# The gathers of segments 5 to 10 issued one segment earlier, in front of the scatters they stood behind

## The chip, the cores and the metric

The kernel runs on one core of a Trainium2 chip. The metric is the device time of one execution in microseconds (us); the median of three runs of the kernel before is 499.98 us (493.82 to 501.89). The core has a matrix engine (TensorE, PE in the profile, with its weight loads as PEld), a vector engine (VectorE, DVE), a scalar engine (ScalarE, ACT), GpSimd (POOL) and a synchronising engine (SP). Each engine works through its own program in order and waits on semaphores for the others. DMA transfers are issued by SP (queue 1 in the profile) and by GpSimd (queue 0) and run beside the engines.

## The reference

Inputs are attention operands q, k, v of shape (4, 8, 576, 64), a router, eight experts and a convolution layer. Cut to what matters:

```python
def reference(...):
    x = windowed_and_dilated_attention(q, k, v)        # (4, 576, 512), 2304 tokens in all
    # MoE: each token has ONE expert e (arg max of x @ w_gate, or the expert of the token before it)
    h = np.maximum(x[b, s] @ w1[e], 0.0)               # w1[e]: 512 x 1024
    out[b, s] = p[e] * (h @ w2[e])                     # w2[e]: 1024 x 512
    # last layer: 5-tap causal convolution as a gate, two 512 x 512 products
    return (sigmoid(conv(out)) * (out @ w_val)) @ w_out
```

Which tokens belong to which expert is only known at run time. So the kernel has to collect the rows of each expert's tokens before the expert's products and to put the results back to the tokens' places afterwards.

## The kernel before, in words

The kernel has three stages: attention with routing (to about 180 us of the profiled execution), the experts (to about 381 us, with the first of them overlapping the attention), and the convolution layer with its two products.

**Segments.** The expert stage is cut into eleven segments, 0 to 10, listed in `SEGS` (line 39) as expert, first slot and number of tokens: 256, 208, 96, 288, 272, 240, 224, 192, 176, 160 and 256 tokens. The loop at lines 1247 to 1282 runs segments 2 to 8; segments 9 and 10 follow it. A segment goes through these steps:

- `gather` (line 305): GpSimd issues one indirect DMA (line 311) for every 128 tokens, from the tensor `xD` in HBM into a tile `xg`. There are four buffers for `xg` (line 220), used in rotation; a buffer is free once TensorE has transposed what it held. Segment 4 has three such tiles, the segments from 5 on have two.
- `turn_x` (line 315): TensorE transposes the tile (line 323, result `xt`), ScalarE and VectorE split it into a high and a low half-precision part, `xh` and `xl` (lines 324, 325).
- `up` (line 328): the first product, eight blocks `h` of three-part sums (line 342), each taken out of PSUM by ScalarE (`hh`, line 344) and VectorE (`hl`, line 346).
- `down` (line 355): the second product, for some tokens by `yf` (line 391, 512 columns) and for the others by `y` (line 375), whose result is turned back by `turn_y` (line 404).
- `send_y` (line 350): ScalarE writes a tile `yr` (three buffers), and GpSimd issues an indirect DMA that scatters its rows into `yD` in HBM (line 353). All scatters write the same tensor `yD`, so each waits on GpSimd for the one ahead of it to land.

**What sets the order.** The order is written out by hand: `up` and `down` are generators that stop after each piece, and the loop counts the pieces with `n` (0 to 7 in `up`, from 8 in `down`) and puts other work between them. In segment g the loop issues the gather of segment g + 1 at n = 0 (line 1254) and transposes it from n = 9 (lines 1270 to 1273), that is in the middle of segment g's `down`. In segment 8 the gather of segment 10 follows that of segment 9 at n = 1, and segment 10 is transposed at the end of the segment (line 1280). The scatters of segment g are issued late in its `down`, just ahead of the next segment's n = 0, so in GpSimd's program each gather stands behind all scatters of the segment before.

**Beside it** run the weights. Eight tiles of 512 KB per expert are fetched by SP into six staging buffers (`wst`, `fetch_w`, line 243) and split by ScalarE (`wh`, line 259) and VectorE (`wl`, line 264), in segment g for segment g + 1; a fetch starts when `wl` has freed its buffer. `late` (from line 1162) prepares the last layer's weights in small steps on VectorE and ScalarE.

Of the kernel before, what the change touches and what calls it, by code (L numbers as in the profile page):

```python
# [157 lines left out]
def attention_moe_conv_kernel(ctx: ExitStack, tc: tile.TileContext, q, k, v, w_gate, w_local, w1, w2, w_val, conv_w, w_out, consts, out):  # L158
# [84 lines left out]
    def fetch_w(k, i, ev):  # L243
        staged.append(staged.pop(0))
        st = staged[-1].tile([P, 1024], F32, tag="wst", name=f"wst{k}_{i}")
        if i < 4:
            nc.sync.dma_start(out=st, in_=w1[bass.ds(ev, 1), i * P : i * P + P, :].rearrange("o p f -> p (o f)"))
        else:
            f0 = (i - 4) * 2 * P
            nc.sync.dma_start(out=st.rearrange("p (a d) -> p a d", a=2), in_=w2[bass.ds(ev, 1), f0 : f0 + 2 * P, :].rearrange("o (a p) d -> p (o a) d", p=P))  # L250
        wf[k, i] = st

    def split_a(k, i):
        w = pools["w1" if i < 4 else "w2"][turn_no[k]]
        st = wf[k, i]
        wh = w.tile([P, 1024], F16, tag="wh", name=f"wh{k}_{i}")
        wl = w.tile([P, 1024], F16, tag="wl", name=f"wl{k}_{i}")
        wt[k, i] = wh, wl
        A.activation(out=wh, in_=st, func=AF.Copy, scale=SW)  # L259

    def split_b(k, i):
        wh, wl = wt[k, i]
        st = wf.pop((k, i))
        V.scalar_tensor_tensor(out=wl, in0=st, scalar=SW, in1=wh, op0=ALU.mult, op1=ALU.subtract)  # L264
# [29 lines left out]
    def tiles_of(n):  # L294
        return [(t0, min(P, n - t0)) for t0 in range(0, n, P)]

    def cols_of(g, which):
        k, t0, n = SEGS[g]
        if k in (0, 2):
            ix = idx[k, t0 > 0][which]  # L300
            return lambda t: ix[:, t : t + 1]
        ix = (idx8, sidx8)[which]
        return lambda t: ix[:, k, t0 + t : t0 + t + 1]

    def gather(g, n=None, col=None, tiles=None):
        if col is None:
            n, col = SEGS[g][2], cols_of(g, 0)
        r = []
        for t0, m in tiles_of(n)[tiles or slice(None)]:
            x = xg.tile([P, D], F32, tag="xg", name=f"xg{g}_{t0}")  # L310
            G.indirect_dma_start(out=x[:m], out_offset=None, in_=xD[0 : 2 * S if g in (0, 1) else N, :], in_offset=bass.IndirectOffsetOnAxis(ap=col(t0 // P)[:m], axis=0))
            r.append(x)
        return r

    def turn_x(g, xs, n=None, pool=None):
        n = n or SEGS[g][2]
        xh = (pool or act).tile([P, 4, n], F16, tag="xh", name=f"xh{g}")
        xl = (pool or act).tile([P, 4, n], F16, tag="xl", name=f"xl{g}")
        xts[g] = (xh, xl)
        for (t0, m), x in zip(tiles_of(n), xs):  # L320
            ps = trp.tile([P, 4, P], F32, tag="tr", name=f"xt{g}_{t0}")
            for cc in range(4):
                T.transpose(ps[:, cc, :m], x[:m, cc * P : cc * P + P], ident[:m, :m])
            A.activation(out=xh[:, :, t0 : t0 + m], in_=ps[:, :, :m], func=AF.Copy, scale=SX)
            V.scalar_tensor_tensor(out=xl[:, :, t0 : t0 + m], in0=ps[:, :, :m], scalar=SX, in1=xh[:, :, t0 : t0 + m], op0=ALU.mult, op1=ALU.subtract)
            yield

    def up(g, k=None, n=None, pool=None, halves=False):
        if n is None:
            k, _, n = SEGS[g]  # L330
        xh, xl = xts.pop(g)
        hh = (pool or pools["h"]).tile([P, 8, n], F16, tag="hh", name=f"hh{g}")
        hl = (pool or pools["h"]).tile([P, 8, n], F16, tag="hl", name=f"hl{g}")
        hts[g] = (hh, hl)
        for fc in range(8):
            fs = slice(fc * P, fc * P + P)
            ps = pools["hp"](f"h{g}_{fc}")
            q = 0
            for cc in range(4):
                wh, wl = wt[k, cc]  # L340
                for w, x in ((wh, xh), (wh, xl), (wl, xh)):
                    T.matmul(ps[:, :n], lhsT=w[:, fs], rhs=x[:, cc, :], start=q == 0, stop=q == 11)  # L342
                    q += 1
            A.activation(out=hh[:, fc, :], in_=ps[:, :n], func=AF.Relu)  # L344
            yield
            V.scalar_tensor_tensor(out=hl[:, fc, :], in0=ps[:, :n], scalar=0.0, in1=hh[:, fc, :], op0=ALU.max, op1=ALU.subtract)  # L346
            if halves:
                yield
# [70 lines left out]
    def drain(g):  # L419
        for _ in g:  # L420
            pass


    if True:
# [554 lines left out]
        vq, xq, evs, xs = [], [], {}, [[], []]  # L979
# [182 lines left out]
    def last_layer(pool):  # L1162
        parts = [(conv_w, KT, None)]
        for src, th, tl, sc in ((w_val, wv_h, wv_l, SVAL), (w_out, wo_h, wo_l, SOUT)):
            parts += [(src[cc * P : cc * P + P, :], P, (th[:, cc, :], tl[:, cc, :], sc)) for cc in range(4)]
        raws = []

        def load(n):
            src, rows, _ = parts[n]
            raw = pool.tile([P, 2 * D if wide else D], I32 if wide else F32, tag="lraw", name=f"lraw{n}", bufs=2)[:rows]  # L1170
            nc.sync.dma_start(out=raw, in_=src.bitcast(I32) if wide else src)
            raws.append(raw)

        load(0)
        for n, (_, rows, to) in enumerate(parts):
            yield
            w32 = raws[n]
            if wide:
                steps = from64(pool, w32, rows, D, f"{n}")
                for m in range(6):  # L1180
                    next(steps)
                    if m == 2 and n + 1 < len(parts):
                        load(n + 1)
                    yield
                w32 = next(steps)
            elif n + 1 < len(parts):
                load(n + 1)
            yield
            if to is None:
                yield  # L1190
                yield
                ps = trp.tile([P, 4, KT], F32, tag="tr", name="cwp")
                for cc in range(4):
                    T.transpose(ps[:, cc, :], w32[:, cc * P : cc * P + P], ident[:KT, :KT])
                V.tensor_copy(out=cw, in_=ps)
                continue
            th, tl, sc = to
            A.activation(out=th, in_=w32, func=AF.Copy, scale=sc)
            yield
            V.scalar_tensor_tensor(out=tl, in0=w32, scalar=sc, in1=th, op0=ALU.mult, op1=ALU.subtract)  # L1200
# [9 lines left out]
    with tc.manual_schedule():  # L1210
# [9 lines left out]
        for t, _ in enumerate(chain(rest_of(first, begun), down(0, pool=pools["y0"]), up(1), down(1)), 45):  # L1220
# [5 lines left out]
            n = t - 45 - sum(at >= 45 for at in UP)  # L1226
# [4 lines left out]
            if t == LAST[1]:  # L1231
                xs3 = gather(3)
# [4 lines left out]
            if t == LAST[3]:  # L1237
                turn = turn_x(2, xs2)
# [4 lines left out]
        r3ctx.close()  # L1243
        last_y = turn_y(1)
        late = last_layer(lw)
        xs = xs3
        for g in range(2, 9):
            kn, kf = SEGS[g + 1][0], SEGS[min(g + 2, 9)][0]
            for n, _ in enumerate(chain(up(g), down(g))):
                if 0 < n < 4:  # L1250
                    next(last_y, None)
                if n in (0, 2, 4) and g == 2:
                    fetch_w(3, 3 + n // 2, evs[3])
                if n == 0 and g > 2:
                    xs = gather(g + 1)
                if n == 1 and g == 8:
                    xs = xs + gather(10)
                if g > 2:
                    if n % 2:
                        split_b(kn, n // 2)  # L1260
                        i = n // 2 + 6
                        if i < 8:
                            fetch_w(kn, i, evs[kn])
                        elif g < 8:
                            fetch_w(kf, i - 8, evs[kf])
                    else:
                        split_a(kn, n // 2)
                for _ in range(LATE[g - 2][n]):
                    next(late, None)
                if n == 9:  # L1270
                    turn = turn_x(g + 1, xs)
                if n in (9, 11, 13):
                    next(turn, None)
                if g == 2 and n == 8:
                    rest()
                if g == 3 and n == 4:
                    weights_of()
            drain(turn)
            if g == 8:
                drain(turn_x(10, xs[2:]))  # L1280
            drain(last_y)
            last_y = turn_y(g)

# [315 lines left out]
```

## Time and profile before

| | |
|---|---|
| median of three runs | 499.98 us (493.82 to 501.89) |
| the profiled execution, its own time | 498.25 us |
| its span, first to last instruction | 496.5 us |
| TensorE busy | 453.8 us, 91% of the span |
| VectorE busy | 350.7 us, 71% |
| ScalarE busy | 296.0 us, 60% |
| GpSimd busy | 164.4 us, 33% |
| moved by DMA | 80.15 MB, mean 161 GB/s |
| mean granted TensorE clock | 0.959 |

The profiled execution is one run of its own; 1.75 us of its time lie outside the span, and it stands 1.7 us below the median of the three runs. TensorE is busy for 91% of the span, so time is either in the amount of its work, in the rate that the granted clock gives it, or in the few places where it stands. The clock has two levels here, full (1.00, which is 2.4 GHz) and half (0.50, 1.2 GHz); a stretch with both shows a number between. "Idle before <- releaser" in a row is the time that the engine stood before that instruction, and what ended it. A row of busy time by stretch gives start:end and length, then busy time and count of PE, PEld, DVE, ACT and POOL, and at its end the granted clock, the DMA share and GB/s.

### The profile page before, as it was taken

How to read it: one execution, taken by the hardware profiler on the slowest of the kernel's cores; microseconds unless marked ns; L12 is line 12 of the kernel's file. 1: busy time of each engine (PE TensorE's matmuls, PEld its weight loads, DVE VectorE, ACT ScalarE, POOL GpSimd, SP SyncE). 2: the span in 40 equal slices, each digit the busy share in tenths (PEclk: the TensorE clock that was granted, in tenths of full speed). 3: DMA queues.
4: the chain of work that ended last, by engine and by line, in shares of the span. 5: the costliest groups of instructions: out<-in, count | busy, mean ns of one | idle time of the engine just before them, and what ended most of it. 6: DMA issues, size and time to landing. Idle time of an engine off the chain costs nothing. (4 is left out here: it accounts for less than half of the span.)

```text
span 496.5 us, 12191 instructions
## 1 busy us (share of the span) xinstructions
PE 453.8 (91%) x4624; PEld 333.8 (67%) x4624; DVE 350.7 (71%) x1013; ACT 296.0 (60%) x597; POOL 164.4 (33%) x183
## 2 busy tenths in 40 slices
PE   6879999888789999999995989898879999999997
PEld 4657677666467478876884878686657675757564
DVE  3667688999878873788895585685914987779840
ACT  5696677867544234456563555575335899786532
POOL 2355555541700252203122131434011483534140
PEclk8699999999979899999999798998989999999999
DMA  8979989866647484276867394964006233111202
GB/s 188 190 168 193 176 205 203 196 146 211 199 130 249 149 287 138 100 208 208 312 219 245 111 296 154 341 207 152 30 9 182 74 118 127 34 69 38 86 0 107
DMA packets 65380, 80.15 MB, mean 161 GB/s; under 512 B 35089, under 2 KB 40225, under 8 KB 65318
## 3 DMA queue, kind: packets, MB, share of 16 engines
q1 hardware_dynamic: 61942, 69.54, 49.4%
q0 software_dynamic: 3232, 9.72, 5.6%
q8 instruction: 38, 0.62, 0.5%
q14 instruction: 24, 0.20, 0.1%
q10 hardware_dynamic: 144, 0.07, 0.1%
HBM read 65.01 MB, written 14.30 MB: 160 GB/s over the span
## 5 line engine op out<-in xcount | busy, mean ns | idle before, releaser
L264 DVE SCALAR_TENSOR_TENSOR wl<-wst,wh 128x1024 f16<-128x1024 f32 x64 | 77.9, 1220 | 18.4 <-ACT wh L259 18.0
L342 PE MATMUL h<-xh,wh 128*128 128x256 f16 (+9 forms) x352 | 87.0, 257 | 3.8 <-DVE hl L346 3.5
L342 PE MATMUL h<-xl,wh 128*128 128x256 f16 (+9 forms) x352 | 86.9, 257 | 0.0
L342 PE MATMUL h<-xh,wl 128*128 128x256 f16 (+9 forms) x352 | 86.9, 257 | 0.0
L342 PEld LDWEIGHTS <-wh 128*128 128x128 f16 x704 | 64.7, 98 | 12.0 <-issue 5.3
L1446 DVE SCALAR_TENSOR_TENSOR acc<-y,cw,acc 128x288 f32<-128x288 f32 x128 | 65.6, 520 | 9.2 <-ACT acc L1420 6.3
L259 ACT ACTIVATE wh<-wst 128x1024 f16<-128x1024 f32 x64 | 67.0, 1050 | 2.1 <-DMA wst<-in_moe_w_dram 2.1
L344 ACT ACTIVATE hh<-h 128x256 f16<-128x256 f32 (+9 forms) x88 | 30.4, 347 | 43.2 <-PE h L342 40.6
L353 POOL DMA_INDIRECT yD<-yr,sidx x15 | 18.2, 1212 | 105.1 <-ACT yr L352 74.9
L556 POOL TENSOR_TENSOR sm<-sm,mx 128x384 f32<-128x384 f32 (+1 forms) x40 | 32.8, 821 | 59.6 <-DVE mx L548 43.2
L346 DVE SCALAR_TENSOR_TENSOR hl<-h,hh 128x256 f16<-128x256 f32 (+9 forms) x88 | 32.0, 375 | 23.8 <-ACT hh L344 23.6
L375 PE MATMUL y<-hh,wh 128*128 128x96 f16 (+6 forms) x288 | 38.8, 209 | 2.2 <-DVEq L1302 2.2
L548 DVE CUSTOM_DVE_ANT_0 sm<-s,cst 128x96 f32<-128x96 f32 x144 | 29.8, 251 | 15.3 <-PE s L540 8.2
L391 PE MATMUL yf<-wl,hh 128*128 128x512 f16 x104 | 40.4, 389 | 0.0
L375 PEld LDWEIGHTS <-wh 128*128 128x128 f16 x576 | 36.6, 104 | 5.6 <-issue 3.5
L391 PE MATMUL yf<-wh,hh 128*128 128x512 f16 x104 | 40.4, 388 | 0.0
L391 PE MATMUL yf<-wh,hl 128*128 128x512 f16 x104 | 40.2, 387 | 0.0
L375 PE MATMUL y<-hl,wh 128*128 128x96 f16 (+6 forms) x288 | 38.6, 209 | 0.7 <-issue 0.7
L540 PE MATMUL s<-kbd,qT 128*64 128x192 f32 x288 | 34.6, 352 | 4.6 <-ACT kbd L524 3.8
L375 PE MATMUL y<-hh,wl 128*128 128x96 f16 (+6 forms) x288 | 38.5, 208 | 0.0
L1476 PE MATMUL v<-yh,wv_h 128*128 128x288 f16 x128 | 36.6, 286 | 0.3 <-DVE gg L1485 0.2
L1476 PE MATMUL v<-yh,wv_l 128*128 128x288 f16 x128 | 36.6, 286 | 0.0
(240 smaller groups left out, 1069.9 us busy)
## 6 DMA issues: line engine op xcount, KB each, us to landing
wst<-in_moe_w_dram SPq DMA_DIRECT2D x64, 512.0 KB
qraw<-in_q_dram SPq DMA_DIRECT2D x16, 288.0 KB
kraw<-in_k_dram SPq DMA_DIRECT2D x16, 288.0 KB
out_dram<-ob SPq DMA_DIRECT2D x17, 256.0 KB
yg<-yD SPq DMA_DIRECT2D x16, 256.0 KB
xD<-xsb SPq DMA_DIRECT2D x2, 1152.0 KB
lraw<-in_moe_w_val_dram SPq DMA_DIRECT2D x4, 512.0 KB
lraw<-in_moe_w_out_dram SPq DMA_DIRECT2D x4, 512.0 KB
```

The lines of the kernel that those rows point to most:

```text
L259: A.activation(out=wh, in_=st, func=AF.Copy, scale=SW)
L264: V.scalar_tensor_tensor(out=wl, in0=st, scalar=SW, in1=wh, op0=ALU.mult, op1=ALU.subtract)
L342: T.matmul(ps[:, :n], lhsT=w[:, fs], rhs=x[:, cc, :], start=q == 0, stop=q == 11)
L344: A.activation(out=hh[:, fc, :], in_=ps[:, :n], func=AF.Relu)
L346: V.scalar_tensor_tensor(out=hl[:, fc, :], in0=ps[:, :n], scalar=0.0, in1=hh[:, fc, :], op0=ALU.max, op1=ALU.subtract)
L375: T.matmul(ps[:, :r], lhsT=w[:, ds_], rhs=x[:, fc, r0:n], start=q == 0, stop=q == 23)
L391: T.matmul(ps, lhsT=x[:, fc, t0 : t0 + P], rhs=w[:, (fc % 2) * D : (fc % 2) * D + D], start=q == 0, stop=q == 23)
L540: T.matmul(ps[64 * half : 64 * half + 64, n, :, :], lhsT=qf[:, QB * blk : QB * blk + QB], rhs=kb[:, bl, :, ks[i] : ks[i] + KB], start=True ...
L548: V.tensor_tensor_reduce(out=sm[:, n, h, :], in0=ps[:, n, h, :], in1=cst[:, o + KB * mi : o + KB * mi + KB], scale=0.125, scalar=-3e38, op ...
L556: G.tensor_tensor(out=smf, in0=smf, in1=mx[:, 0 : 2 * ns].unsqueeze(2).to_broadcast([P, 2 * ns, KB]), op=ALU.subtract)
L1446: V.scalar_tensor_tensor(out=acc, in0=y32[:, cc, s0 + k : s0 + k + hw], scalar=cw[:, cc, k : k + 1], in1=acc, op0=ALU.mult, op1=ALU.add)
L1476: T.matmul(ps, lhsT=w[:, cc, cs], rhs=x[:, cc, hs], start=q == 0, stop=q == 11)
```

## The change

The list `xs` becomes a queue of gathered segments. The gather of segment 4 stays at the start of segment 3. From then on, at n = 7 of segment g (the last piece of its `up`), the gather of segment g + 2 is issued and put at the end of the queue; `turn_x` takes from its front. So the gathers of segments 5 to 10 are issued one segment earlier than before, and the separate gather of segment 10 in segment 8 goes.

```diff
-        xs = xs3
+        xs = [xs3]
         for g in range(2, 9):
             ...
-                if n == 0 and g > 2:
-                    xs = gather(g + 1)
-                if n == 1 and g == 8:
-                    xs = xs + gather(10)
+                if n == 0 and g == 3:
+                    xs.append(gather(4))
+
+                if n == 7 and g > 2:
+                    xs.append(gather(g + 2))
             ...
                 if n == 9:
-                    turn = turn_x(g + 1, xs)
+                    turn = turn_x(g + 1, xs.pop(0))
             ...
             if g == 8:
-                drain(turn_x(10, xs[2:]))
+                drain(turn_x(10, xs.pop(0)))
```

The programs of TensorE, VectorE, ScalarE and SP keep their order; GpSimd's alone changes. The first place is in segment 3, where the moved gathers begin. In the names, `xg5_0` is the first tile of segment 5's gather, `yr3_256` the tile from token 256 of segment 3 that is scattered into `yD`; the number behind the last underscore only tells instances apart. Before:

```order
L311 DMA xg4_256_3638<-xD_57,idx8_113 16x512
L353 DMA yD_58<-yr2_0_3663,sidxb_2908 2305x512
L353 DMA yD_58<-yr3_0_3953,sidxb_2908 2305x512
L353 DMA yD_58<-yr3_256_4007,sidxb_2908 2305x512
L353 DMA yD_58<-yr3_128_4023,sidxb_2908 2305x512
L311 DMA xg5_0_4047<-xD_57,idx8_113 128x512
L311 DMA xg5_128_4049<-xD_57,idx8_113 112x512
L353 DMA yD_58<-yr4_128_4357,sidx8_114 2305x512
```

With the change:

```order
L311 DMA xg4_256_3638<-xD_57,idx8_113 16x512
L353 DMA yD_58<-yr2_0_3663,sidxb_2908 2305x512
L311 DMA xg5_0_3796<-xD_57,idx8_113 128x512
L311 DMA xg5_128_3798<-xD_57,idx8_113 112x512
L353 DMA yD_58<-yr3_0_3957,sidxb_2908 2305x512
L353 DMA yD_58<-yr3_256_4011,sidxb_2908 2305x512
L353 DMA yD_58<-yr3_128_4027,sidxb_2908 2305x512
L311 DMA xg6_0_4188<-xD_57,idx8_113 128x512
L311 DMA xg6_128_4190<-xD_57,idx8_113 96x512
L353 DMA yD_58<-yr4_128_4361,sidx8_114 2305x512
```

Segment 5's gather has moved in front of the three scatters of segment 3, and where it stood there is now the gather of segment 6. The same shift holds for every segment up to the end of the loop. The second place is that end, in GpSimd's program at segments 7 and 8. Before:

```order
L353 DMA yD_58<-yr7_128_5391,sidx8_114 2305x512
L353 DMA yD_58<-yr7_0_5409,sidx8_114 2305x512
L311 DMA xg9_0_5432<-xD_57,idx8_113 128x512
L311 DMA xg9_128_5434<-xD_57,idx8_113 32x512
L311 DMA xg10_0_5454<-xD_57,idx8_113 128x512
L311 DMA xg10_128_5456<-xD_57,idx8_113 128x512
L353 DMA yD_58<-yr8_128_5720,sidx8_114 2305x512
```

With the change:

```order
L311 DMA xg9_0_5229<-xD_57,idx8_113 128x512
L311 DMA xg9_128_5231<-xD_57,idx8_113 32x512
L353 DMA yD_58<-yr7_128_5395,sidx8_114 2305x512
L353 DMA yD_58<-yr7_0_5413,sidx8_114 2305x512
L311 DMA xg10_0_5560<-xD_57,idx8_113 128x512
L311 DMA xg10_128_5562<-xD_57,idx8_113 128x512
L353 DMA yD_58<-yr8_128_5720,sidx8_114 2305x512
```

Segment 9's gather has moved in front of segment 7's scatters; segment 10's gather keeps its place but has no other gather in front of it.

## Rows read from the trace of the kernel before

**Rows 1.** Waits of TensorE, 200 to 375 us: total us, times, longest us

```profile
PE xt L323 <- DMA xg<-xD,idx: 11.7, 4, 5.5
...
PE h L342 <- DVE hl L346: 2.1, 4, 0.8
```

**Rows 2.** Timeline of TensorE around the longest wait: start us, us, instruction

```profile
273.17 1.09 PE L323 MATMUL xt<-cst,xg 128*128 128x128 f32 x4 [5.55 <-DMA xg<-xD,idx]
```

**Rows 3.** Busy time by stretch, the four waits: start:end length, busy per engine

```profile
267.62:273.17 5.55, 0.01 (x1) 0.03 (x1) 0.00 (x1) 0.26 (x1) 1.45 (x2) 0.84 0.77 269
296.16:298.23 2.07, 0.00 (x0) 0.03 (x1) 0.21 (x1) 0.25 (x1) 0.00 (x0) 1.00 1.02 301
318.34:320.30 1.96, 0.00 (x0) 0.03 (x1) 0.00 (x0) 0.22 (x1) 0.00 (x0) 1.00 0.88 327
337.40:339.52 2.12, 0.00 (x1) 0.03 (x1) 0.13 (x1) 0.21 (x1) 1.82 (x2) 1.00 0.71 238
```

**Rows 4.** Timeline of GpSimd, segments 3 to 6

```profile
224.31 1.00 POOL L353 DMA_INDIRECT yD<-yr,sidxb  x1 [16.38 <-ACT yr L352]
...
235.15 0.98 POOL L311 DMA_INDIRECT xg<-xD,idx  x1 [0.30 <-issue]
...
259.21 1.74 POOL L353 DMA_INDIRECT yD<-yr,sidx  x1 [5.36 <-ACT wh L259]
265.77 0.99 POOL L353 DMA_INDIRECT yD<-yr,sidx  x1 [4.82 <-ACT wh L259]
267.06 1.08 POOL L311 DMA_INDIRECT xg<-xD,idx  x1 [0.30 <-issue]
...
290.30 2.02 POOL L311 DMA_INDIRECT xg<-xD,idx  x1 [0.31 <-PE h L342]
```

**Rows 5.** The gathers' tile xg, 180 to 400 us: from issue to landing

```profile
DMA to landing us min/median/max: 2.5/5.6/7.8
```

**Rows 6.** Busy time by stretch: after three waits, then undisturbed pieces of like work

```profile
273.17:278.22 5.05, 5.05 (x49) 4.99 (x50) 1.13 (x2) 1.81 (x3) 0.00 (x0) 0.50 0.00 0
298.23:302.09 3.86, 3.86 (x47) 3.82 (x48) 0.69 (x1) 1.79 (x3) 0.00 (x0) 0.56 0.33 125
320.30:320.77 0.47, 0.47 (x4) 0.46 (x5) 0.00 (x0) 0.00 (x0) 0.00 (x0) 1.00 0.57 218
339.52:343.03 3.51, 3.51 (x59) 3.32 (x59) 1.01 (x2) 1.85 (x4) 0.08 (x1) 0.51 0.42 124
266.28:267.46 1.18, 1.18 (x25) 1.18 (x23) 1.18 (x2) 0.00 (x0) 0.88 (x2) 1.00 0.76 191
302.83:303.86 1.03, 1.03 (x27) 1.03 (x26) 1.03 (x2) 0.38 (x1) 0.00 (x0) 1.00 0.00 0
336.64:337.25 0.61, 0.61 (x25) 0.61 (x23) 0.61 (x1) 0.00 (x0) 0.33 (x1) 1.00 1.03 423
```

**Rows 7.** Busy time by stretch: segments 5, 6, 7, 8, and eight crowded us

```profile
253.74:282.92 29.18, 23.63 (x229) 20.07 (x228) 17.95 (x28) 14.24 (x26) 5.70 (x6) 0.88 0.61 210
282.92:306.88 23.96, 21.78 (x229) 18.51 (x228) 16.73 (x27) 13.55 (x25) 5.70 (x5) 0.93 0.70 220
306.88:326.48 19.60, 17.59 (x230) 14.43 (x229) 14.30 (x22) 12.46 (x24) 6.60 (x5) 1.00 0.80 276
326.48:347.48 21.00, 18.75 (x237) 15.51 (x236) 14.16 (x20) 13.52 (x27) 8.31 (x7) 0.92 0.58 193
...
312.00:320.00 8.00, 6.34 (x73) 4.80 (x71) 6.01 (x10) 4.16 (x8) 5.07 (x3) 1.00 1.00 341
```

**Rows 8.** Busy time by stretch: segment 4, whose successor's gather was early

```profile
229.74:253.74 24.00, 24.00 (x233) 19.39 (x232) 20.67 (x33) 15.09 (x27) 5.07 (x5) 1.00 0.69 238
```

**Rows 9.** Timeline of TensorE: segment 4's first transposes, in segment 3

```profile
220.17 0.64 PE L323 MATMUL xt<-cst,xg 128*128 128x128 f32 x4
```

**Rows 10.** Timeline of VectorE: one weight split that frees a buffer

```profile
305.29 1.22 DVE L264 SCALAR_TENSOR_TENSOR wl<-wst,wh 128x1024 f16<-128x1024 f32 x1 [1.00 <-ACT wh L259]
```

**Rows 11.** Timeline of ScalarE: the use of the tile fetched into that buffer

```profile
315.48 1.06 ACT L259 ACTIVATE wh<-wst 128x1024 f16<-128x1024 f32 x1
```

## The prediction

> **What bounds the kernel now.** I read the waits of TensorE first, over the expert segments, because that engine is busy almost throughout and what it waits for is what the end waits for. It has one large item: 11.7 us in four waits for the gathers' tile `xg`, the longest 5.5 us [rows 1]. The next item that the change could touch, four waits for `hl`, is 2.1 us. The timeline shows where the longest lies: the transpose at 273.17, the first piece of `turn_x` for segment 6 in the middle of segment 5 [rows 2].
>
> Then I asked what the other engines did in these four stretches. Over the 5.55, 2.07, 1.96 and 2.12 us VectorE worked 0.00 + 0.21 + 0.00 + 0.13 = 0.34 us and ScalarE 0.26 + 0.25 + 0.22 + 0.21 = 0.94 us [rows 3]. So the whole core stands for the gather, and neither engine brings a backlog that would become the next wait.
>
> Why the gather is late is in GpSimd's timeline [rows 4]. The scatters of segment 4 start at 259.21 and 265.77, over six us apart, since each waits for the one ahead to land. (The releasers printed there, `wh` of ScalarE, had long been done; these are put down to the wrong engine.) The gather of segment 6 stands behind them and starts at 267.06, and gathers take 5.6 us to land in the median, 7.8 at most [rows 5]. 267.06 + 5.6 = 272.7, and TensorE goes on at 273.17. It had been ready for it at 267.62.
>
> A wait costs more than its length. After three of the four the granted clock is at or near its half level (1.2 GHz) for a while: means of 0.50, 0.56 and 0.51, against 1.00 after the third wait, at 320.30 [rows 6].
>
> **The change, step by step.** The same DMAs are issued; none is added or taken away. The programs of the four other engines keep their order, so only the times at which the gathers are issued and land can differ.
>
> *The waits.* With the change the gather of segment 6 stands where that of segment 5 stood, at 235.15 [rows 4], and is needed at 267.62: 32 us ahead against at most 7.8 needed. The gather of segment 7 takes the place at 267.06, needed at 296.16; that of segment 8 the place at 290.30, needed at 318.34; that of segment 9 takes a place one segment ahead in the same way. All four waits go: 5.55 + 2.07 + 1.96 + 2.12 = **11.7 us**. Segment 4 is the control in the same trace: the gather that it transposes was also issued well ahead, and TensorE is busy there for 24.00 of 24.00 us at a clock of 1.00 [rows 8].
>
> *The clock.* Half rate is priced by like work at full rate. In segment 5, 24 `y` matmuls of 112 columns take 1.18 us [rows 6], 0.0492 us each. The stretch after the wait holds 49 matmuls, four of them transposes: 45 x 0.0492 = 2.2 us. A group of four transposes takes 0.47 us at 1.00 [rows 6]. So 2.7 us of work took 5.05: 2.35 lost. In segment 6: 42 matmuls of 96 columns at 1.03 / 24 = 0.0429 us, with 0.47 for the transposes, 2.3 us against 3.86: 1.6 lost. (Of the 47 counted four are transposes and one lies over the edge.) In segment 8: 50 of 48 columns at 0.61 / 24 = 0.0254 us and two groups of transposes, 1.27 + 0.94 = 2.2 against 3.51: 1.3 lost. Sum **5.2 us**. Bounds: 0 if the clock falls all the same, and 5.2, as no more is lost there. I take 5.2: in segment 4, with no wait, the clock stayed up.
>
> The Trainium skill has another price for this: "TensorE: Matmul & The Clock Gate", in its terms for `throttle_active`, puts the penalty at the throttled time times one minus the clock ratio, that is half of it. By that the three stretches would give back 0.50 x 5.05 + 0.44 x 3.86 + 0.49 x 3.51 = 5.9 us and the sum would be 0.7 us larger. The rows say less, since matmuls of 48 columns did not take twice as long at half the clock.
>
> *The wait that is added.* `xg` has four buffers. Segment 4's gather holds three, so the second tile of segment 5's needs one that is freed by the transpose at 220.17, which ends at 220.81 [rows 9]. GpSimd stands there until then, and behind it the first scatter of segment 3. That one started at 224.31, when ScalarE had written its `yr` [rows 4]; the two us that a gather's issue takes at most (2.02 at 290.30) end by 222.9. Nothing is paid, and if this cover of 1.4 us went, that scatter would start late by as much and be followed by a gather that has tens of us. From segment 4 on a gather needs only the two buffers that the segment before has freed.
>
> *The transfers.* Segments 5 to 8 must move the same bytes in less time. Length x GB/s gives 6.13, 5.27, 5.41 and 4.05 MB [rows 7]. The shorter lengths are 29.18 - 5.55 - 2.35 = 21.3, 23.96 - 2.07 - 1.6 = 20.3, 17.6 and 21.00 - 2.12 - 1.3 = 17.6 us, so the rates become 288, 260, 307 and 230 GB/s. The trace shows 341 over eight us with a DMA share of 1.00 [rows 7]. Price 0; the cover is that margin, and the distance of a weight tile from its use: the shortest I found is from the split that frees the buffer (305.29 + 1.22 = 306.51) to ScalarE's use of the new tile at 315.48, 9.0 us [rows 10, 11]. That stretch contains no wait on a gather and does not get shorter.
>
> *VectorE* has 17.95, 16.73, 14.30 and 14.16 us of work in the four segments [rows 7], under each of the shorter lengths, by 3.3 us or more. Price 0. It would be the next bound.
>
> **Sum.** 11.7 + 5.2 = 16.9 us. Against the profiled execution's 498.25 us this is 481.3; against the median of the three runs, 1.7 us higher, 483.1. The three runs lie 8 us apart, and I cannot tell which part of that is in these waits. I say **482**.
>
> **Rivals.**
>
> *The transfers bite.* The waits moved bytes too: 269, 301, 327 and 238 GB/s while TensorE stood [rows 3]. The Trainium skill warns of this in "DMA: Bandwidth & Descriptors", section "Issuing engines are not separate DMA queues": transfers of all issuers run on the same 16 engines and interleave, so an early gather adds no bandwidth. As a mechanism here: if no segment could keep more than 250 GB/s, a level between those of the four segments (193 to 276), they would last 24.5, 21.1, 21.6 and 17.6 us, 3.2 + 0.8 + 4.0 = 8 us of the gain would come back, and the time is **490**. The 341 GB/s speak against it. Chance 0.09.
>
> *The clock stays low.* The waits go, the half-rate stretches stay: 11.7 us, **487**. For it: the rows do not say what the clock follows. Against: segment 4 and the third wait. Chance 0.08.
>
> *The change does not do what it says.* The gather's buffer is not free when its turn comes, GpSimd waits for a transpose of the following segment, and the gather lands as late as before: **499**. The rotation of four buffers speaks against it, since only one tile of segment 5 meets this. Chance 0.05.
>
> *Slower.* A weight tile comes late: the moved gather and the scatters are in flight when the six staging buffers refill, ScalarE stands at `wh`, behind it in its program stand `hh` and then TensorE. It decides from a landing time above 9.0 us [rows 10, 11], and to be worse than before by 10 us the tiles would have to cost 27 us in four segments, 6.7 each, so land some 16 us after the issue. No wait of ScalarE for a tile shows in these segments. Price at that point **510**. Chance 0.03.
>
> **How the numbers follow.** My forecast has 0.75. Two per cent of 499.98 is 10 us, about what a measurement of this kernel tells from no change, so "faster" means under 490. It holds the forecast nearly whole (0.73), the clock rival (0.08) and half of the transfer rival: 0.85. "Same" has the other half, the case that nothing moves and a rest: 0.12. "Slower" is the last rival, 0.03. Range: 478 to 490 takes in the forecast with some 4 us of scatter between runs on its lower side, the clock rival at 487 and the edge of the transfer rival.
>
> **What would show it.** In the profile after, TensorE's waits have no item `xt <- xg`, or under 1 us. The granted clock is 1.00 in segments 5 to 8, and these last about 21.3, 20.3, 17.6 and 17.6 us. GpSimd's gathers stand ahead of a segment's scatters and land before they are asked for. From segment 9 on every length stays as it was. I am wrong if a wait of TensorE for `xh`, `hl` or a weight tile appears where `xt` waited, if ScalarE waits for `wst`, or if the clock falls in these segments without a wait.

## The result and the profile after

| | before | after |
|---|---|---|
| median, four runs each on one chip | 498.86 us (493.82 to 501.89) | 480.82 us (480.53 to 484.93) |
| the same two kernels in a second set of runs | 501.46 us (497.44 to 502.59, 7 runs) | 484.96 us (482.3 to 486.48, 4 runs) |
| the profiled execution, its span | 498.25 us, 496.5 us | 480.95 us, 479.2 us |
| mean granted TensorE clock | 0.959 | 0.968 |

The ratio is 0.969 with a 95% interval of 0.9591 to 0.979, in the second set of runs 0.967 (0.9609 to 0.9731). The change saves 16.5 to 18 us, about 3%; 482 was forecast. (The median before is 499.98 us over three runs and 498.86 over four.) Against what the title says, the gathers issued a segment earlier are those of segments 5 to 9 alone: segment 10's stands behind segment 7's scatters and ahead of segment 8's in both kernels.

Where the time came from is read in the same order as before. First the waits of TensorE in the profile after, 190 to 360 us (total us, times, longest us):

```profile
PE y L375 <- DVEq L1303: 2.2, 1, 2.2
PE h L342 <- DVE hl L346: 2.0, 4, 0.8
PE y L375 <- issue: 0.5, 1, 0.5
```

The item `xt <- xg` of [rows 1] is gone and nothing has taken its place; what stands here was there before, all of it in segment 9: four waits for `hl`, and a stop of 2.2 us (2.2 before too) at a loop whose number of passes is known only at run time (line 1303; nothing of its body shows in the trace), with a short one behind it. Then busy time by stretch after the change: segments 5, 6, 7 and 8, and segment 4 as the control (start:end length, then busy time and count of PE, PEld, DVE, ACT, POOL; granted clock, DMA share, GB/s):

```profile
254.16:275.25 21.09, 21.09 (x229) 17.69 (x228) 18.00 (x28) 14.23 (x26) 5.88 (x6) 1.00 0.84 271
275.25:295.37 20.12, 20.02 (x230) 16.88 (x228) 16.75 (x27) 13.45 (x25) 5.26 (x5) 1.00 0.86 278
295.37:312.75 17.38, 17.38 (x230) 14.37 (x229) 14.30 (x22) 12.48 (x24) 6.51 (x5) 1.00 0.92 309
312.75:330.17 17.42, 17.29 (x237) 14.24 (x236) 14.16 (x20) 13.43 (x27) 5.95 (x5) 1.00 0.61 216
230.16:254.16 24.00, 24.00 (x233) 19.39 (x232) 20.66 (x33) 15.09 (x27) 4.83 (x5) 1.00 0.73 237
```

Against [rows 7] the four segments shrank from 93.74 us (253.74 to 347.48) to 76.01 (254.16 to 330.17), by 17.73, at a clock of 1.00 throughout, and TensorE is now busy for all but 0.23 us of them. Segment 4 is as long as in [rows 8]. The rest did not move: segment 5 starts 0.42 us later, and from the start of segment 9 to the end it is 149.02 us before (496.5 - 347.48) and 149.03 after (479.2 - 330.17). So the whole gain lies in segments 5 to 8: 17.73 - 0.42 = 17.3 us, the difference of the two spans.

Third, GpSimd's timeline after the change, segments 3 to 5 (start us, us, instruction, idle before and its releaser):

```profile
221.51 0.94 POOL L311 DMA_INDIRECT xg<-xD,idx  x1 [11.89 <-PE xt L323]
224.74 1.00 POOL L353 DMA_INDIRECT yD<-yr,sidxb  x1 [2.29 <-ACT yr L352]
...
235.57 0.98 POOL L311 DMA_INDIRECT xg<-xD,idx  x1 [0.31 <-issue]
...
259.54 1.84 POOL L353 DMA_INDIRECT yD<-yr,sidx  x1 [5.26 <-ACT wh L259]
266.49 0.99 POOL L353 DMA_INDIRECT yD<-yr,sidx  x1 [5.12 <-ACT wh L259]
267.78 1.16 POOL L311 DMA_INDIRECT xg<-xD,idx  x1 [0.30 <-issue]
```

The scatters keep their distance of almost seven us (259.54, 266.49), as in [rows 4]. But the gather behind them at 267.78 is now that of segment 7, wanted at 288.33. Segment 6's has gone out at 235.57, 32.3 us ahead of its transpose at 267.89. At 221.51 stands the one wait that the change adds: segment 5's second tile waits 11.89 us for the buffer that segment 4's first transpose frees. The scatter behind it still waits for `yr`, for 2.29 us after that gather's issue, so it is not held up.

The stretches that answer to [rows 6], from the first transpose to the second, in segments 5, 6 and 8:

```profile
267.89:270.70 2.81, 2.81 (x57) 2.80 (x54) 0.89 (x2) 1.84 (x4) 1.98 (x2) 1.00 0.91 290
288.33:290.92 2.59, 2.59 (x57) 2.50 (x54) 1.06 (x3) 1.76 (x4) 0.00 (x0) 1.00 0.96 306
323.52:325.29 1.77, 1.77 (x59) 1.72 (x55) 0.75 (x2) 1.31 (x4) 0.00 (x0) 1.00 0.94 366
```

No stretch at 0.50 to 0.56 is left there: the clock is 1.00 and TensorE is busy for the whole of each.

### The profile page after: what moved, and what is told of

It reads as the page before. It is cut to its first block, busy times and chain, and to the rows that moved or that the text cites. A ratio compares the mean times of both kernels' runs of the same rounds, so it can differ in the third digit from the quotient of the medians.

```text
span 479.2 us, 12191 instructions
## 1 busy us (share of the span) xinstructions
PE 449.5 (94%) x4624; PEld 330.0 (69%) x4624; DVE 350.0 (73%) x1013; ACT 296.4 (62%) x597; POOL 163.3 (34%) x183
## 5 line engine op out<-in xcount | busy, mean ns | idle before, releaser
L342 PEld LDWEIGHTS <-wh 128*128 128x128 f16 x704 | 64.5, 98 | 11.8 <-issue 5.3
L540 PE MATMUL s<-kbd,qT 128*64 128x192 f32 x288 | 35.6, 361 | 4.5 <-ACT kbd L524 3.8
L375 PEld LDWEIGHTS <-wh 128*128 128x128 f16 x576 | 33.0, 98 | 5.3 <-issue 3.3
L375 PE MATMUL y<-hh,wh 128*128 128x96 f16 (+6 forms) x288 | 34.6, 199 | 2.2 <-DVEq L1303 2.2
L1477 PE MATMUL v<-yl,wv_h 128*128 128x288 f16 x128 | 36.6, 286 | 0.0
L342 PEld LDWEIGHTS <-wl 128*128 128x128 f16 x352 | 34.5, 98 | 2.6 <-issue 0.2
```

Of the source, the lines that this page charges most:

```text
L375: T.matmul(ps[:, :r], lhsT=w[:, ds_], rhs=x[:, fc, r0:n], start=q == 0, stop=q == 23)
L540: T.matmul(ps[64 * half : 64 * half + 64, n, :, :], lhsT=qf[:, QB * blk : QB * blk + QB], rhs=kb[:, bl, :, ks[i] : ks[i] + KB], start=True ...
L1477: T.matmul(ps, lhsT=w[:, cc, cs], rhs=x[:, cc, hs], start=q == 0, stop=q == 11)
```

## Experiments

The experiments ran in two sets. The kernel before had a median of 500.58 us (13 runs) in the first, to which belong the two halves, the gather ahead of the last scatter and the run with TensorE kept busy; it had 501.46 us (7 runs) in the second, with the other three. The changed kernel ran in the second alone, so in the first its profile above stands in for it. Since the stage ahead varies from run to run (below), stages are compared by their lengths.

The theory is the prediction's: a gather is late only because it stands behind scatters on GpSimd, each wait belongs to its own gather, and three of the four waits also cost clock. The rivals: the gain is one train of delays set off by the first wait; transfers take it back; the half clock has another cause.

### The gathers of segments 5 and 6 alone

Against the kernel before, with `xs` as the change's queue:

```diff
-                if n == 0 and g > 2:
-                    xs = gather(g + 1)
+                if n == 0 and g == 3:
+                    xs.append(gather(4))
+                if n == 7 and g in (3, 4):
+                    xs.append(gather(g + 2))
+                if n == 0 and g > 5:
+                    xs.append(gather(g + 1))
                 if n == 1 and g == 8:
-                    xs = xs + gather(10)
+                    xs.append(gather(10))
```

> Only the gathers of segments 5 and 6 are issued one segment early; those of 7, 8, 9 and 10 stand behind the scatters as before. Theory (each gather's lateness is made in its own segment): the wait of 5.55 us in segment 5 and its half-clock stretch go, the three waits of 2.07, 1.96 and 2.12 us stay within 0.5 us; the segments 6, 7 and 8 keep their lengths of before (24.0, 19.6, 21.0) and the time is 8 us under before, about 491. Rival one (the first wait causes the later ones): all four go, 481. Rival two (the time only moves on): the later waits grow by what the first gave, 497 to 499.

Measured: 491.19 us (490.02 to 494.78, 4 runs), ratio 0.9815 (0.9757 to 0.9873). TensorE's wait for `xt` in this run, 190 to 360 us, and the stretches behind its three main stops (1.71, 2.14 and 1.94 us, ahead of the transposes at 295.63, 316.27 and 335.65):

```profile
PE xt L323 <- DMA xg<-xD,idx: 6.2, 4, 2.1
```

```profile
295.63:298.23 2.60, 2.60 (x53) 2.51 (x53) 0.69 (x1) 1.52 (x3) 0.00 (x0) 1.00 0.66 252
316.27:318.30 2.03, 2.03 (x52) 1.90 (x52) 0.73 (x2) 1.26 (x3) 0.00 (x0) 1.00 0.81 291
335.65:339.50 3.85, 3.85 (x81) 3.71 (x82) 1.97 (x3) 2.13 (x5) 0.26 (x1) 0.62 0.43 127
```

The long wait in segment 5 went, and the three waits of segments 6 to 8 stayed within 0.4 us of [rows 3]. Segments 5 to 8 took 83.99 us (21.09 + 21.99 + 20.11 + 20.80) in place of 93.74: 9.75 gained. The waits of the later segments are not the first one's echo. Of the three stops only the last was followed by a lowered clock (0.62). So one part of the expectation failed: segment 6 did not keep its 24.0 us, mostly because the clock stayed at 1.00 behind its stop, where [rows 6] has 0.56.

### The other half: gathers 5 and 6 late, 7 to 10 early

Against the kernel before, with the same queue:

```diff
-                if n == 0 and g > 2:
-                    xs = gather(g + 1)
-                if n == 1 and g == 8:
-                    xs = xs + gather(10)
+                if n == 0 and g in (3, 4, 5):
+                    xs.append(gather(g + 1))
+                if n == 7 and g > 4:
+                    xs.append(gather(g + 2))
```

> The opposite: the gathers of segments 5 and 6 stand where they stood before, those of 7 to 10 are early. Theory: one wait of TensorE for the gather remains, 5.5 us in segment 5, the clock falls to half after it and nowhere else in segments 5 to 8; 8 us over the changed kernel, about 489. This and the run with only 5 and 6 early should then add up to the whole gain: 8 + 9.6 = 17.7. Rival (the first wait causes the later ones): the waits of segments 6 to 8 come back too, 495 or more.

Measured: 493.42 us (493.08 to 493.72), ratio 0.9868 (0.9813 to 0.9923). The wait, and segments 5 and 6:

```profile
PE xt L323 <- DMA xg<-xD,idx: 6.3, 1, 6.3
```

```profile
256.31:286.10 29.79, 23.45 (x229) 19.88 (x228) 17.95 (x28) 14.25 (x26) 8.45 (x8) 0.89 0.68 214
286.10:306.21 20.11, 20.01 (x229) 16.88 (x228) 16.73 (x27) 13.45 (x25) 6.05 (x5) 1.00 0.87 268
```

Segment 5 is as slow as before, segments 6 to 8 are as short as with the whole change (20.11, 17.37 and 17.43 us). The four take 84.70 us, 9.04 gained. The halves add up but for 1 us: 9.75 + 9.04 = 18.8 against 17.73 for the whole, above all because segment 6 kept its clock in both halves, so that this gain counts twice; by the medians it is 9.4 + 7.2 = 16.6 against 16.5 to 18. Each gather's lateness is made and paid in its own segment. The time is 4 us above the expected 489, and the profiled run (493.25 us) says where: against the profile of the changed kernel segment 5 starts 2.15 us later, the four segments take 8.7 us more and not 8 (the wait is 6.3 us in place of 5.55), and from segment 9 on it is 1.5 us longer.

### The order before, with scatters that don't wait for each other

```diff
+    yDs = [yD] + [dram.tile([N + 1, D], F32, name=f"yD{n}") for n in (1, 2)]
-        G.indirect_dma_start(out=yD[:, :], ...)
+        G.indirect_dma_start(out=yDs[t0 // P][:, :], ...)
...
-        nc.sync.dma_start(out=g[:m], in_=yD[...])
+        nc.sync.dma_start(out=g[:m], in_=xD[...])
```

> The order before the change. The scatters of a segment's first, second and third tile go to tensors of their own, so that a scatter no longer waits for the transfer of the one just ahead of it; the last layer reads xD in place of yD, so the experts' result is left out of the output, and nothing after the loop waits for a scatter. No gather is moved. Theory (a gather is late only because it stands behind scatters that wait for each other): the scatters come 1 to 2 us apart in place of 6.5, the gather of segment 6 starts at about 257 us of a run whose segment 5 starts at 254, some 10 us earlier than before, its rows land 4 us before they are wanted, all four stops of TensorE for xt go, and segments 5 to 8 take 76 to 78 us in place of 93.7: 481 to 484 us in all. Rival 1 (a gather has to be issued a whole segment ahead because transfers beside it hold it up): stops of 1 us and more stay at segments 6 to 9, which take 85 to 94 us. Rival 2 (the clock falls for a reason other than these stops): no stops, yet granted clock of 0.5 at the starts of segments 6, 7 and 9, some 81 us.

Measured: 486.13 us (485.29 to 487.06), ratio 0.9707 (0.9655 to 0.9758), beside 484.96 for the changed kernel in the same set. GpSimd from segment 5's start (257.69 in this run) on:

```profile
256.42 1.37 POOL L354 DMA_INDIRECT yD<-yr,sidx  x1 [17.66 <-ACT yr L353]
258.10 0.88 POOL L354 DMA_INDIRECT yD<-yr,sidx  x1 [0.30 <-issue]
259.28 1.01 POOL L354 DMA_INDIRECT yD<-yr,sidx  x1 [0.30 <-issue]
260.60 2.01 POOL L312 DMA_INDIRECT xg<-xD,idx  x1 [0.30 <-issue]
```

and segments 5 to 8 by stretch:

```profile
257.69:278.77 21.08, 21.08 (x230) 17.70 (x228) 18.00 (x28) 14.30 (x26) 5.79 (x6) 1.00 0.80 278
278.77:299.86 21.09, 20.03 (x229) 16.88 (x228) 16.86 (x27) 13.44 (x25) 4.36 (x5) 1.00 0.81 263
299.86:317.24 17.38, 17.38 (x229) 14.37 (x228) 14.30 (x22) 12.47 (x24) 6.06 (x5) 1.00 0.91 311
317.24:334.67 17.43, 17.30 (x238) 14.24 (x237) 14.16 (x20) 13.42 (x27) 9.51 (x7) 1.00 0.68 235
```

With no gather moved, the scatters stand 1.2 to 1.7 us apart and segment 6's gather starts 2.9 us after segment 5 does, in place of 13.3. All stops for `xt` are gone, the clock is 1.00, and the four segments take 76.98 us. (Segment 6 has a new stop of 1.06 us for `hl`, whose cause is open.) This settles the cause: it was the scatters waiting for each other, not the transfers and not the distance of a segment. Segment 6's gather was issued 10.8 us ahead of its transpose (260.60, 271.41) and came in time; how long it took can't be read, since this trace has the landing of only one gather behind 190 us.

### The gather ahead of the last scatter only

Against the changed kernel (in segment 8 the place stays):

```diff
-                if n == 7 and g > 2:
+                if n == (14 if g < 8 else 7) and g > 2:
                     xs.append(gather(g + 2))
```

> The smallest step that takes a gather out of the scatters' chain: it stands ahead of the LAST scatter of a segment only, some 5 us earlier in GpSimd's program than before, and not a segment (segment 10's gather stands as in the changed kernel). Theory (the lateness is the last scatter's wait for the one ahead to land): in segment 5 the gather starts at about 261.3 instead of 267.1 and lands 5.6 us later, so that 0 to 1.5 us of the wait remain; in segments 6, 7 and 8 it starts 6.5 us earlier and no wait remains. 481 to 484. Rival (a gather needs most of a segment because of the transfers beside it): waits of 1 us and more remain in three or four segments, 488 or more.

Measured: 484.8 us (484.41 to 486.13), ratio 0.9703 (0.9647 to 0.9759). In segment 4 (segment 5 starts at 256.04 in this run) GpSimd now has the gather between its second and its last scatter:

```profile
261.49 1.74 POOL L353 DMA_INDIRECT yD<-yr,sidx  x1 [5.37 <-ACT wh L259]
263.53 1.07 POOL L311 DMA_INDIRECT xg<-xD,idx  x1 [0.30 <-issue]
267.19 1.22 POOL L353 DMA_INDIRECT yD<-yr,sidx  x1 [1.19 <-ACT hh L344]
```

It is wanted at 269.76, 6.2 us after its issue, and TensorE does not stop for it or for any later one. Segments 5 to 8 take 77.69 us, 1.68 more than after the change, all in segments 7 and 8, whose waits (297 to 334 us) and lengths, with one crowded stretch, are

```profile
PE h L342 <- DVE wl L264: 0.5, 1, 0.5
PE y L375 <- DVE hl L346: 0.4, 1, 0.4
PE h L342 <- DVE hl L346: 0.3, 1, 0.3
```

```profile
297.23:315.04 17.81, 17.54 (x230) 14.38 (x229) 14.36 (x22) 12.47 (x24) 4.42 (x5) 1.00 0.86 305
315.04:333.73 18.69, 17.66 (x238) 14.36 (x237) 14.26 (x20) 13.41 (x27) 6.85 (x7) 1.00 0.63 217
...
317.00:325.00 8.00, 7.40 (x82) 6.16 (x80) 5.27 (x9) 4.40 (x10) 3.99 (x4) 1.00 1.01 357
```

Passing one scatter is enough to end the four stops. What remains is three small waits, one for a weight split (`wl`) and two for `hl`; the one for `wl` stands in a stretch with 357 GB/s at a DMA share of 1.01 for eight us. That may be the transfer rival of the prediction, but it isn't shown: the changed kernel has a stretch just as crowded in segment 7, and TensorE was busy for all of it.

```profile
298.00:306.00 8.00, 8.00 (x81) 6.52 (x79) 7.47 (x13) 5.49 (x11) 5.03 (x3) 1.00 1.03 357
```

The cause of these 1.7 us is open.

### Keeping TensorE busy through the waits

```diff
-    def turn_x(g, xs, n=None, pool=None):
+    def turn_x(g, xs, n=None, pool=None, fill=0):
...
+            for _ in range(fill if t0 == 0 else 0):
+                w = wt[SEGS[g - 1][0], 4][0]
+                T.matmul(..., lhsT=w[:, 0:P], rhs=w[:, 0:512], start=True, stop=True)
...
-                    turn = turn_x(g + 1, xs)
+                    turn = turn_x(g + 1, xs, fill={5: 23, 6: 8, 7: 7, 8: 8}.get(g, 0))
```

> The kernel before, its order kept; ahead of the first transpose of segments 6, 7, 8 and 9 TensorE runs 23, 8, 7 and 8 matmuls of 512 columns whose result is thrown away (about 0.215 us each: 4.9, 1.7, 1.5 and 1.7 us), so it works through the waits for the gather. The gathers land no earlier. Theory (the idle time takes the clock down, and a stop costs a drain besides): the granted clock stays at 1.00 in segments 5 to 8, the waits shrink to 0.2 to 0.8 us each, and the time falls by the clock's part of the gain alone, 5 to 6 us, to about 493. Rival (the half rate comes from something else at this place, the transposes or the landing of the gather): the stretches at half rate stay, no change, 499.

Measured: 500.74 us (498.57 to 503.67, 10 runs), ratio 1.0004 (0.9968 to 1.0039): no change, where 493 was expected. TensorE's remaining wait, 240 to 360 us, and the stretches from the first transpose to the second in segments 5 to 8:

```profile
PE xt L326 <- DMA xg<-xD,idx: 4.1, 4, 1.4
```

```profile
277.26:280.11 2.85, 2.85 (x52) 2.84 (x53) 0.69 (x1) 1.57 (x3) 0.00 (x0) 1.00 0.01 4
300.73:303.36 2.63, 2.63 (x52) 2.54 (x53) 0.69 (x1) 1.51 (x3) 0.00 (x0) 1.00 0.41 164
321.78:323.76 1.98, 1.98 (x52) 1.92 (x52) 0.66 (x2) 1.19 (x3) 0.00 (x0) 1.00 0.71 265
341.99:343.78 1.79, 1.79 (x52) 1.74 (x53) 0.47 (x1) 1.10 (x3) 0.00 (x0) 1.00 0.41 142
```

The clock part of the theory holds: with only stops of 0.53 to 1.45 us left (0.2 to 0.8 were expected), the clock stays at 1.00, and from the first transpose to the next segment it takes 7.41, 7.08, 6.10 and 6.67 us against 9.75, 8.65, 6.18 and 7.96 before, 5.3 us less. The expected time failed all the same. The four segments lost only 2.96 us, because their gathers came 0.0, 0.75, 0.55 and 1.07 us later after the segment's start, though issued at the same distance from it: TensorE could go on only 8.7, 7.1 and 7.5 us after the issue, where it was 7.9, 6.6 and 6.4 before. Why is open. The rest lies outside these segments: segment 5 starts 4.1 us later than in the profile before, and from segment 9 on it is 1.6 us longer, so that the profiled run is 2.8 us slower than the one before. 3.0 gained and 1.6 lost would leave 1.4 us, which the interval of the ten runs (1.6 us faster to 2.0 slower) can't tell from nothing.

### The changed kernel again, and a version with late work moved

The control is the changed kernel itself:

> The changed kernel once more, as the control for the two runs beside it. Both theories expect its first result again: 481 us (within 1), segments 5 to 8 together 76 us (21.1, 20.1, 17.4, 17.4), and no stop of TensorE for xt in them.

It took 484.96 us: segments 21.68, 20.11, 17.38 and 17.42, together 76.59, and no stop for a gather (a stop of 0.4 us for `yT` in segment 5 is new). It is 4 us above its first median and outside the expected 481 within 1. Between the two profiled runs (480.95 and 485.53) 3.7 of the 4.6 us lie ahead of segment 4, as the last section shows, 0.6 in segment 5 and 0.3 behind segment 8.

The other takes up VectorE, which the prediction named the next bound. In the first 13.83 us of segment 9 its work (12.66 us, after the change) is ahead of TensorE's (10.04):

```profile
330.17:344.00 13.83, 10.04 (x110) 7.82 (x107) 12.66 (x30) 4.42 (x12) 0.99 (x1) 1.00 0.09 28
```

```diff
-LATE = (..., (0, 0, 0, 0, 0, 1, 0, 0, 0, 0, 1, 0, 0, 0, 0, 1), (0, 0, 0, 0, 0, 0, 0, 1, 0, 0, 0, 0, 0, 0, 0, 1))
+LATE = (..., (0, 0, 0, 0, 0, 1, 0, 0, 0, 1, 1, 0, 1, 0, 0, 1), (0, 0, 0, 0, 0, 0, 0, 1, 1, 1, 0, 1, 1, 0, 1, 1))
```

> The changed kernel, with segments 7 and 8 given 5 and 7 of the late steps in place of 3 and 2, so that 7 of these steps (about 0.57 us of VectorE each, 4 us in all) leave the stretch at the start of segment 9, which took 13.8 us at 12.7 us of VectorE and 10.0 us of TensorE. Theory (with the gathers early, TensorE bounds segments 7 and 8 and VectorE has 3 us to spare in each, so that VectorE's stretch at segment 9 is the next bound): that stretch takes 10 to 11 us, segments 5 to 8 stay at 76 to 77 us, and the whole takes 478 us, 2 to 3 us below the changed kernel. Rival (VectorE's and the transfers' work in segments 7 and 8, whose transfers ran at 309 GB/s, has no room): these segments grow by the 2 to 4 us that segment 9 gives back, 481 us or more.

Measured: 484.06 us (481.02 to 487.97), ratio 0.969 (0.9611 to 0.9768): not to be told from the control, neither 478 nor slower. The piece of 13.83 us ends at no event of TensorE, so the whole of segment 9 is compared, first with the change alone and then in this run:

```profile
330.17:351.73 21.56, 16.82 (x223) 12.35 (x220) 12.72 (x31) 7.18 (x19) 1.86 (x2) 0.92 0.06 20
330.87:351.79 20.92, 16.79 (x223) 12.16 (x220) 9.77 (x24) 7.17 (x19) 1.87 (x2) 0.92 0.05 18
```

TensorE's waits from 254 to 360 us, and VectorE's first instruction behind the loop of line 1303:

```profile
PE h L342 <- DVE hl L346: 2.2, 5, 1.2
PE yf L391 <- ACT warm L1513: 2.1, 1, 2.1
```

```profile
343.22 0.06 DVE L1357 MEMSET warm<- 128x1 f32 x1 [2.11 <-issue]
```

Segments 5 to 8 took 76.74 us, so they had room for the steps, and 2.95 us of VectorE's work did leave segment 9; but the segment became only 0.6 us shorter (1.0 against the control's 21.88), where 3 to 4 were expected of its first piece. The `hl` waits stayed (2.0 us in segment 9, and 0.2 in segment 8), and so did the stop at the loop: 2.2 us with VectorE's queue as its releaser after the change, here 2.1 us, to 343.74, though VectorE had been idle from 341.1 to 343.22. So VectorE's total was not the bound there; what sets this stop is open.

## Why the prediction was right

*The waits: 11.7 predicted, 12.3 measured.* From a segment's start to its first transpose it took 19.43, 15.31, 13.42 and 13.04 us before, and 13.73, 13.08, 11.29 and 10.77 after: 5.70 + 2.23 + 2.13 + 2.27 = 12.33. That is 0.15 to 0.17 more than the printed wait in each. The sum lacked a term, which the rows at the transpose show, the first before and the others after the change:

```profile
267.41 0.21 PE L375 MATMUL y<-hh,wl 128*128 128x112 f16 x1
267.84 0.21 PE L375 MATMUL y<-hh,wl 128*128 128x112 f16 x1
267.89 0.61 PE L323 MATMUL xt<-cst,xg 128*128 128x128 f32 x4
```

The row of a `y` matmul is 0.21 us long, but without a stop the transpose starts 0.05 after the last `y` has started. The printed wait is counted from that row's end, so a stop costs 0.16 us more than its printed length. (The ends of these rows are the profile's model.)

*The clock: 5.2 predicted, 5.3 measured.* From the first transpose to the next segment it took 9.75, 8.65, 6.18 and 7.96 us before, and 7.36, 7.04, 6.09 and 6.65 after: 2.39 + 1.61 + 0.09 + 1.31. The 0.09 is segment 7's, whose clock was 1.00 in both; the other three make 5.31. The terms of like work (2.35, 1.6, 1.3) were right to 0.04 us, and the run with fillers found 5.3 by another way. Here the profiled execution was lucky for the forecast: in the first half alone a stop of 1.71 us in segment 6 cost no clock, so the 1.6 and 1.3 us need not be there in every execution. The Trainium skill's rule in "TensorE: Matmul & The Clock Gate" (the terms for `throttle_active`), by which half of the throttled time is lost, gave an estimate of 5.9; the rows decide for the smaller number, 5.3.

*The sum.* 16.9 predicted, 17.7 in the four segments, 17.3 between the profiled executions. The lengths 21.1, 20.1, 17.4 and 17.4 stand against 21.3, 20.3, 17.6 and 17.6, the 0.2 in each being for the most part the missing 0.16. That 482 lies between the medians of the two sets, 480.82 and 484.96, is in part luck: they are 4 us apart, and the prediction could not tell where such a scatter lies.

*The added wait: 0.* The issue after it at 221.51 ended at 222.45 and the scatter behind it started at 224.74, against 224.31 before, in a run whose segment 4 also starts 0.42 us later (230.16, 229.74): unmoved.

*The transfers: 0.* The rates are 271, 278, 309 and 216 GB/s where 288, 260, 307 and 230 were worked out, no weight tile was late, and the gathers landed after 5.8 us in the median, 7.7 at most, as in [rows 5]. Where the change puts the gathers there was room. Signs of a limit, both unexplained, are the 1.7 us of the run with the gather ahead of the last scatter and the later gathers of the run with fillers. The Trainium skill states in "DMA: Bandwidth & Descriptors", section "Issuing engines are not separate DMA queues", that transfers of all issuers interleave on the same 16 engines; no run here isolates what one issuer's transfers cost another's.

*VectorE: 0.* 18.00 us of work in a segment of 21.09 left no wait for it.

*The rivals.* The clock did not stay low; all four waits went; nothing came late that had been in time. What the prediction left open, which part of the scatter between runs lies in these waits, stays open for the kernel before, of which there is one profile; the changed kernel has none of these waits, and its runs still lie between 480.53 and 486.48 us.

## What to carry to other kernels

When an engine waits for a transfer, ask in the issuing engine's program what the issue stands behind: here 5.6 us of transfer were late only because of scatters that each waited for the one ahead, and moving the issue ahead of them or letting them not wait gave nearly the same, 17.7 and 16.8 us in the four segments. Price a stop of TensorE with its printed length, the overlap of rows that it breaks (0.16 us here), and, where the clock falls behind it, like work at the lower clock. A cure for the clock alone gave 3 us in these segments, since the gathers then came later, and nothing that the medians could show.

## What the runs showed of the hardware

**The clock does not follow a stop's length alone.** Stops of 1.71 and 2.14 us (first half alone) and of 1.96 us (before) were followed by a clock of 1.00; stops of 1.94 us (first half alone, 0.62 behind it) and of 2.07 and 2.12 us (before) by half clock. The stops of 5.55 us (before) and 6.34 us (the other half, 0.54 behind it) were both followed by it, the four of 0.53 to 1.45 us in the run with fillers were not. So a term for the clock of a two-us stop is uncertain in either direction.

**Most of the spread between the profiled runs lies ahead of the change.** Segment 4 starts at 229.74 us before, at 230.16 after, and between 230.13 and 235.59 in the other seven profiled runs, with the same programs up to there but for GpSimd's order in segment 3 and, in one, the scatters' targets. Between the two profiles of the changed kernel it is 3.67 us: 2.07 are there already at the same transpose of the attention stage (105.36 and 107.43), and 1.60 come in segment 2, in the first

```profile
193.05:202.75 9.70, 9.61 (x205) 9.40 (x204) 7.67 (x25) 4.73 (x15) 3.92 (x5) 1.00 0.33 104
```

and in the second

```profile
195.11:206.41 11.30, 10.39 (x205) 9.63 (x204) 7.73 (x25) 4.50 (x15) 3.87 (x5) 1.00 0.28 89
```

with the same instructions at the same clock; 0.8 of the 1.6 us are idle time of TensorE (10.39 and 9.61 us busy). The kernel before had 9.71 us there, the other six runs 11.1 to 11.3, so the two profiles of the main comparison share the short form. Behind segment 8 the nine runs differ less, by 2.2 us (148.4 to 150.6). What decides between 9.7 and 11.3 was not tried.
